# Sparse attention in front of a gated MLP: the probability transposes of 28 jobs on VectorE instead of TensorE, with the scores laid out for it

## The chip, the cores and the metric

The kernel runs on one core of a Trainium2 chip. The core has TensorE (PE in the profile; PEld is its loading of weights), VectorE (DVE), ScalarE (ACT), GpSimd (POOL) and SyncE (SP), which issues most DMAs. Each engine works through its own queue in order. The metric is the device time of one execution in microseconds; the kernel before takes 769.71 us (median of three runs, 769.57 to 770.93).

## The reference

Block-sparse attention over 4 batches, 8 heads, 768 positions and a head dimension of 64, in blocks of 32 positions (24 blocks). Its output feeds an MLP with 512 inputs, 2048 hidden values and a gate `h * relu6(h + 3) / 6`.

```python
scores = scale * np.matmul(q, k.transpose(0, 1, 3, 2))
mask = np.abs(blk_i - blk_j) <= window                     # window = 1 block
mask = mask | (blk_i == 0) | (blk_j == 0) | (blk_i == n_blocks - 1) | (blk_j == n_blocks - 1)
...                                                        # and 3 sampled blocks for each query block
scores = np.where(mask, scores, -1000000000.0)
attn = np.exp(scores - np.max(scores, axis=-1, keepdims=True))
attn = attn / (np.sum(attn, axis=-1, keepdims=True) + 1e-09)
attn_out = np.matmul(attn, v)
...
h = x @ w_in
out = (h * np.clip(h + 3.0, 0.0, 6.0) / 6.0) @ w_out
```

An inner query block sees at most eight key blocks (its neighbours and itself, the first and the last, three sampled). The first and the last query block see all 24.

## The kernel before

**Units of work.** `GROUPS` holds 24 groups: two halves of the batch times 12 pairs of query blocks. Eleven groups of each half are inner pairs; each gives a `Cache` (its eight key and value blocks, loaded into one of two buffers `KP`, `VP`) and two `Job`s, one for each batch of the half: 44 jobs, 22 caches. The remaining group of each half holds the first and the last block and gives four `Dense` jobs. A job makes 64 rows of the MLP's input; eight jobs (four groups) fill 512 tokens, a unit of the MLP. Each unit has 16 `Step`s, one per 128 hidden values, 96 steps in all.

**A job before** (lines 452 to 534). A job has two query blocks `x`, four pairs of heads `t` and the two heads `y` of a pair.

- `s` (462): scores. For each `x`, `t`, `y` one fp32 matmul puts 32 queries times 256 keys (eight key blocks, called slots) into PSUM bank `ps[y]`, at partitions `32t` and columns `256x`: 16 matmuls. In the trace each fp32 matmul is two instructions, `bank<-kp,q`, 64 rows by 32 columns of the array and 256 columns wide.
- `mx` (472): the row maximum, one VectorE reduction for each `y`.
- `e` (479): the exponential on ScalarE, four of them, with the maximum as its bias. It reads slot after slot and writes the columns in the order key within block, slot (`c k s`), so that the transposed tile mixes four slots in one group of 128.
- `t` (486): four 128x128 transposes on TensorE into another PSUM bank (`bank<-ident,p`), for each `y`.
- `ca` or `cv` (491, 495): ScalarE or VectorE copies that to SBUF (`pT`).
- `av` (499): probabilities times values, 16 matmuls for each `y` (`small<-vp,pT`, two instructions each, 128 rows by 32 columns, 65 wide: 64 values and a column of ones that gives the sum).
- `dn`, `ml`, `x` (511 to 523): the reciprocal of the sum, the product, and a VectorE transpose of 32x32 blocks. `xh`, `xl` split the result into a high and a low part for the MLP.

The values of a cache are stored to match: row `4k + s` of `VP` holds key `k` of slot `s` (`values`, 388, `slot % 4::4`).

**A step** (658 to 709). `wh`, `wl` split 128 rows of each weight into a rounded part and the rest (ScalarE, then GpSimd or VectorE). `h` makes the hidden values in two halves of six 128x512 matmuls (`hid`), `ga` (ScalarE), `gb` (VectorE), `gh` (ScalarE) and `gl` (GpSimd) the gate and its split, `o` twelve 128x512 matmuls into the four output banks `OUT`. `hid` has one bank.

**PSUM** has two banks `bank`, one `hid`, one `small` and four `OUT`. The jobs of the first four groups (`early`) also use the `OUT` banks. Scores and transposes of later jobs share the two banks.

**The order** is written out in `SCORE`, a list of phrases such as `j32 s; j33 s; j32 mx_0`: a work, and the operations to issue for it. Every instruction is kept in that order on its engine (`Ordered`, 308; all instructions are recorded there, so the profile shows L316 for nearly all of them). The weights come as 64-bit numbers and are converted by `Weight` (`w` phrases) during the first unit.

Of the kernel before, what the change touches and what calls it, by code (L numbers as in the profile page):

```python
# [10 lines left out]
F32 = mybir.dt.float32  # L11
# [6 lines left out]
P = 128  # L18
# [16 lines left out]
EARLY = 4  # L35
WBUFS = (3, 2)
# [8 lines left out]
    k0 samp_1; q1 load_0; k0 table_1; c0 kg_0; q0 load_1; c1 vw_01; c0 kw_11 vg_0; w1 load_1; c0 kr_111 kr_001; c1  # L45
    kw_11 vw_00 kf_0; c0 vw_01 kw_00; c1 kc_1; k0 index; w0 load_0; c1 kr_000; w1 size; q0 qs_0; c1 kr_010; c0 vw_02
    vw_00; k0 ident_0; c0 vr_01; j1 s; j0 s; j1 mx_0; c0 vr_00; j1 mx_1; c2 kc_0; j0 mx_0; w0 size; j0 mx_1; j1 e_00;
    c1 vr_00; w0 bits_0; j0 e_00 e_01; j1 e_01; j0 e_10; c1 vw_02; j0 e_11; q1 qs_0; w2 load_0; c2 kr_010; j2 s; j0
    t_0 t_1; c2 kr_000; j0 cv_0 ca_1; j1 t_0; j0 av_0; j1 e_10 cv_0 e_11; j0 av_1; j2 mx_0; c2 kw_01; j3 s; j0 dn; j2
    e_00; j0 ml; j2 e_01 mx_1; j1 t_1; c3 kw_01; j3 mx_0; j2 t_0; c1 vg_0; w0 bits_1; q2 load_0; j1 av_0; j2 ca_0; c1  # L50
    vr_01; j3 mx_1; j2 e_10; j1 cv_1; j3 e_00; j2 e_11; w1 bits_0; j1 av_1; j3 e_01; w1 bits_1; w2 size; j2 t_1; c2
    vw_00; w0 bits_2; c3 kr_010; j2 ca_1; j1 dn; j0 x; j3 e_10; j1 ml; w1 bits_2; j1 x; q3 load_0; c2 vw_02; q2 qs_0;
    w4 load_0; m0 wh_0; j4 s; c2 vr_01; j3 e_11; m0 wl_00; j1 xh; m0 wh_1; j2 av_0; j1 xl_1; c2 vw_01; j0 xh; j5 s; c3
    kc_1; c2 vr_00; w2 bits_0; j3 t_0; j5 mx_0; c3 kr_000; j3 t_1; j0 xl_1; j5 e_00; j2 av_1; j4 mx_0 e_00; j2 dn; q3
    qs_0; j2 ml; q4 load_0; j3 ca_0 cv_1; j4 e_01; j3 av_0; w2 bits_1; w4 size; j3 av_1; j2 x; j5 e_01; m0 wl_11; j4
    t_0; c3 vw_00; j4 mx_1; c4 kw_01; j4 ca_0; w3 load_0; j3 dn; j4 e_10; c3 vr_01; w2 bits_2; j4 e_11; j3 ml; j4 t_1;
    j5 mx_1; j4 av_0; c3 vw_01; j4 cv_1; j5 t_0; c3 vw_02; j3 x; c3 vr_00; j6 s; j5 e_10; j2 xh; j5 e_11; j2 xl_0; j5
    ca_0; j4 av_1; c4 kw_00; j6 mx_0; c4 kr_000; j5 t_1; w4 bits_0; j6 e_00; j4 dn; j6 e_01; j7 s; j5 cv_1; j3 xh; w3
    size; j6 mx_1 t_0; c4 kr_010; j4 ml; j6 e_10; j3 xl_1; j5 av_0; j6 ca_0; j7 mx_0; j6 e_11; j5 av_1; w3 bits_0; j7
    e_00; w3 bits_1; j7 e_01; w6 load_0; j7 t_0; w3 bits_2; j6 t_1; j5 dn; j7 mx_1; j4 x; j7 e_10; w4 bits_1; j6 ca_1;  # L60
    q4 qs_0; j5 ml; w4 bits_2; j6 av_0; j7 ca_0; j6 av_1; j5 x; j7 e_11; w5 load_0; j4 xh; j7 t_1; c5 kw_00; j6 dn; j5
    xh; j4 xl_0; c4 vw_01; j6 ml; j7 ca_1; j8 s; w7 load_0; j5 xl_0; j6 x; m1 wh_0; c4 vw_02 vw_00; j7 av_0; j6 xh; m1
    wl_00; j8 mx_0; c4 vr_00; m2 wh_0; j7 av_1; j8 e_00; j7 dn; j8 e_01; j7 ml; j8 t_0; c4 vr_01; j7 x; j6 xl_1; j7
    xh; w6 size; j7 xl_1; j8 mx_1; m0 h_0; w5 size; j8 e_10; w5 bits_0; j8 e_11; w6 bits_0; m0 h_1; m1 wh_1; j8 cv_0;
    m1 wl_11; j8 t_1; m0 ga; w6 bits_1; j8 ca_1; w6 bits_2; j9 s; m0 gb; w9 load_0; q5 load_0; w5 bits_1; m0 gh; m1
    h_0; c5 kw_01; w5 bits_2; w7 size; m0 gl; j9 mx_0; w8 load_0; m1 h_1; c5 kr_000; m2 wl_01; j9 e_00 e_01; w7
    bits_0; m0 o_0; m1 ga; j8 av_0; m1 gb; w9 size; j8 av_1; c5 kr_010; j9 mx_1; m3 wh_0; j9 t_0; m2 h_0; w7 bits_1;
    m3 wl_00; j9 e_10 e_11; w7 bits_2; m1 gh; m0 o_1; m1 gl; m2 h_1; w9 bits_0; w10 load_0; c5 vw_00 vw_01; m0 o_2; j8
    dn; m2 ga; w9 bits_1; m0 o_3; w8 size; w9 bits_2; j9 t_1 ca_0; m1 o_0; j8 ml; w11 load_0; q5 qs_0; j9 cv_1; c5
    vr_01; m1 o_1; w8 bits_0; j10 s; m2 gb; c6 kw_00; m2 gh; j9 av_0; c5 vw_02; j10 mx_0; m2 wh_1; j9 av_1; m2 gl; c5  # L70
    vr_00; j10 mx_1; m1 o_2; w10 size; w8 bits_1; j10 e_00; m1 o_3; j10 e_01; m2 wl_11; j10 e_10; m3 h_0; j10 e_11; w8
    bits_2; w10 bits_0; m4 wh_0; w12 load_0; m3 h_1; j8 x; w11 size; w10 bits_1; j10 t_0; m4 wl_01; m3 ga; m2 o_0; w10
    bits_2; j10 t_1; j9 dn; w14 load_0; m2 o_1; w11 bits_0; j10 ca_1; m3 gb; m2 o_2; j8 xh; j10 ca_0; w11 bits_1; m4
    h_0; m5 wh_0; j9 ml; w11 bits_2; m3 wh_1; j11 s; m3 gh; w13 load_0; c6 kr_010; m3 gl; j10 av_0; j11 mx_0; j10
# [219 lines left out]
def fused_kernel(ctx: ExitStack, tc, qT, kG, vG, vP, kD, vD, sampled, w_in, w_out, table, ident_d, out):  # L294
# [488 lines left out]
```

## Time and profile before

| | |
|---|---|
| median of three runs | 769.71 us |
| the profiled execution | 768.11 us, its span 766.3 us |
| PE / PEld / DVE / ACT / POOL busy | 724.3 / 558.4 / 341.7 / 426.4 / 360.7 us |
| mean granted TensorE clock | 0.994 |
| moved by DMA | 102.52 MB, mean 134 GB/s |
| first `hid` matmul starts at | 70.04 us |
| last matmul ends at | 761.3 us |

The profile gives the busy time of each engine, the span in 40 equal slices (each digit a busy share in tenths), the chain of work that ended last, and groups of instructions: line, engine, operation, what it writes and reads, shapes, count, busy time and the mean duration in ns, then the idle time before them and what ended it. Matmuls overlap, so their durations are longer than their spacing: what one costs is read from the start of one to the start of the next. A timeline row holds start, length, engine, operation and count of instructions merged into one row.

### The profile page before, as it was taken

To read this page: it belongs to the slowest core of one execution; us is meant where nothing else is said; L and a number is where in the kernel's file an instruction comes from. 1 tells how busy PE (TensorE), PEld (TensorE's weight loads), DVE (VectorE), ACT (ScalarE), POOL (GpSimd) and SP (SyncE) were. 2 spreads that over 40 slices of the span, in tenths; PEclk is the share of its full clock that TensorE was granted. 3 is DMA by queue.
4 is the path that set the end of the run, shared out by engine and by line. 5 is a ranking of instruction groups with operands and counts; after the bars stand their busy time and mean duration, and the time that the engine had idled before them with its cause. 6 is when DMAs were issued, how large, how long until landed. Compare 5 with 4: busy or idle time off the path is not lost.

```text
span 766.3 us, 18861 instructions
## 1 busy us (share of the span) xinstructions
PE 724.3 (95%) x7616; PEld 558.4 (73%) x7616; DVE 341.7 (45%) x698; ACT 426.4 (56%) x790; POOL 360.7 (47%) x291
## 2 busy tenths in 40 slices
PE   1577999999999999999999999999999999999997
PEld 0344777777777777777778777777777777888885
DVE  2567989895443434542323334436642133221112
ACT  1567678766565445645656554455654645544441
POOL 0011324355446434455664663442546564676663
PEclk9989999999999999999999999999999999999999
DMA  8688878776361553223451144533442600010001
GB/s 281 199 274 253 284 232 246 239 249 198 122 197 62 169 176 124 64 74 115 153 161 58 35 138 129 179 131 106 133 142 86 207 20 2 1 56 1 0 1 55
DMA packets 57866, 102.52 MB, mean 134 GB/s; under 512 B 7859, under 2 KB 36148, under 8 KB 57780
## 3 DMA queue, kind: packets, MB, share of 16 engines
q1 hardware_dynamic: 56512, 99.62, 41.3%
q10 hardware_dynamic: 1268, 1.71, 0.6%
q8 instruction: 60, 0.98, 0.5%
q14 instruction: 26, 0.21, 0.1%
HBM read 95.00 MB, written 6.29 MB: 132 GB/s over the span
## 4 chain that ended last, share of the span: by engine, by line
PE 89%; SPq 4%; DMA 2%; DVE 2%; ACT 1%; issue 1%; ACTq 0%; POOL 0%; POOLq 0%; DVEq 0%
PE hid L316 35%; PE out L316 34%; PE bank L316 12%; PE small L316 8%; SPq L316 3%; DMA stage<-w_out 1%; ACT p L316 1%; SPq L370 1%; DVE m L316 0%; DMA stage<-w_in 0%; DMA kp<-kG 0%; ACT g L316 0%; DMA vp<-vG 0%; DMA out_dram<-stage 0%; DVE w_in L316 0%
## 5 line engine op out<-in xcount | busy, mean ns | idle before, releaser
L316 PE MATMUL hid<-x,whi 128*128 128x512 f32 x768 | 242.9, 397 | 0.3 <-ACT x L316 0.2
L316 POOL TENSOR_TENSOR glo<-g,ghi 128x512 fp32r<-128x512 f32 x96 | 126.5, 1318 | 181.8 <-ACT ghi L316 163.6
L316 DVE SCALAR_TENSOR_TENSOR g<-g,hid 128x512 f32<-128x512 f32 x96 | 65.8, 686 | 229.8 <-ACT g L316 229.8
L316 PEld LDWEIGHTS hid<-x,whi 128*128 128x128 f32 x768 | 140.6, 188 | 34.6 <-issue 3.2
L316 POOL TENSOR_TENSOR wlo<-w_out,whi 128x512 fp32r<-128x512 f32 x87 | 113.7, 1308 | 98.0 <-ACT whi L316 78.3
L316 PE MATMUL out<-whi,ghi 128*128 128x512 f32 x384 | 159.7, 416 | 0.0
L316 ACT ACTIVATE p<-bank,m 128x256 f32<-128x256 f32 (+1 forms) x192 | 120.8, 691 | 65.1 <-DVE m L316 64.5
L316 POOL TENSOR_TENSOR wlo<-w_in,whi 128x512 fp32r<-128x512 f32 x87 | 113.4, 1308 | 84.3 <-ACT whi L316 79.7
L316 PE MATMUL out<-whi,glo 128*128 128x512 f32 x384 | 150.5, 392 | 0.2 <-POOL glo L316 0.2
L316 PE MATMUL hid<-x,wlo 128*128 128x512 f32 x384 | 150.2, 391 | 0.0
L316 PE MATMUL out<-wlo,ghi 128*128 128x512 f32 x384 | 150.0, 391 | 0.0
L316 ACT ACTIVATE g<-hid,half_b 128x512 f32<-128x512 f32 x96 | 66.1, 688 | 122.8 <-PE hid L316 93.1
L316 DVE TENSOR_REDUCE m<-bank 128x2 f32<-128x512 f32 (+1 forms) x112 | 70.3, 645 | 61.0 <-PE bank L316 60.9
L316 PEld LDWEIGHTS out<-whi,ghi 128*128 128x128 f32 x384 | 72.1, 188 | 22.9 <-issue 9.5
L316 PEld LDWEIGHTS out<-whi,glo 128*128 128x128 f32 x384 | 72.1, 188 | 16.5 <-POOL glo L316 0.6
L316 PEld LDWEIGHTS hid<-x,wlo 128*128 128x128 f32 x384 | 72.1, 188 | 15.8
L316 PEld LDWEIGHTS out<-wlo,ghi 128*128 128x128 f32 x384 | 72.4, 189 | 11.6
L316 ACT CAST whi<-w_out 128x512 fp32r<-128x512 f32 x96 | 60.0, 625 | 32.5 <-PE out L316 29.2
L316 ACT CAST ghi<-g 128x512 fp32r<-128x512 f32 x96 | 60.0, 625 | 31.9 <-DVE g L316 17.2
L316 ACT CAST whi<-w_in 128x512 fp32r<-128x512 f32 x96 | 59.6, 624 | 12.9 <-PE hid L316 8.3
L316 PE MATMUL bank<-ident,p 128*128 128x128 f32 x384 | 58.2, 274 | 2.0 <-ACT p L316 1.7
L316 PEld LDWEIGHTS small<-vp,pT 128*32 128x32 f32 x2816 | 42.6, 110 | 22.9 <-issue 15.3
(59 smaller groups left out, 607.4 us busy)
## 6 DMA issues: line engine op xcount, KB each, us to landing
vp<-vG SPq DMA_DIRECT2D x176, 130.0 KB, 3.4
kp<-kG SPq DMA_DIRECT2D x129, 128.0 KB, 2.8
kp<-kG SPq DMA_DIRECT2D x42, 256.0 KB, 3.6
stage<-w_in SPq DMA_DIRECT2D x16, 512.0 KB, 3.9
stage<-w_out SPq DMA_DIRECT2D x15, 512.0 KB, 4.3
vp<-vP SPq DMA_DIRECT2D x26, 260.0 KB, 3.9
stage<-vD SPq DMA_DIRECT2D x16, 390.0 KB, 4.0
out_dram<-stage SPq DMA_DIRECT2D x24, 256.0 KB, 2.9
```

The lines of the kernel that those rows point to most:

```text
L316: return lambda *a, **k: tc.keep_in_program_order(op(*a, **k))
L370: loads, values = nc.values_load_multi_w_load_instructions(row, engines=[engines[q]], min_val=0, max_val=NB - 1, skip_runtime_bounds_check ...
```

## The change

For jobs 16 to 43 (`n >= TURNED`, 16) the layout of the scores is another. The four slots of a half `c` no longer lie side by side in a row, but on the four groups of 32 partitions: `spread` puts the scores of slots `r` and `r + 4` (`r` from 0 to 3) at partitions `32r` and columns `64(4x + t)`, 32 keys of each slot in their order. A matmul is then 64 columns wide and there are 64 for each job. VectorE's transpose works on blocks of 32x32, so that one instruction for each `y` (`tr`) turns 128x512 probabilities into the layout that `av` needs. The transposes on TensorE, their PSUM bank and the copies `ca`, `cv` are gone for these jobs. The row maximum now spans four groups of partitions: `ms` reduces each group with one operand, `mc` brings the four together with seven small minima (of negated maxima) and spreads the result, `sb` adds it on VectorE from PSUM to SBUF, and `ex` is an exponential in place, without bias, one for each `y`.

The values of their caches (8 to 21) lie in slot order: row `32s + k`. A block pair that was one DMA (`vw_1`, `vg`) is two there.

Jobs 0 to 15 keep the transposes on TensorE. Their score matmuls write the permuted order `c k s` into PSUM (a stride of four elements) and the exponential reads and writes contiguous columns.

`SCORE` is written anew throughout, from its first phrase on. The counts of other operations change little: 11 and 12 of the 96 splits of `w_in` and `w_out` are on VectorE instead of 9 and 9, and three query scalings are on GpSimd instead of one.

```diff
+TURNED = 16
...
         def values(self, slot, step=4):
+            if self.turned:
+                return self.v[slot % 4 * BLK:slot % 4 * BLK + BLK, slot // 4]
             return self.v[slot % 4::step, slot // 4]
+
+        def pair(self, q, slot, pair):
+            if self.turned:
+                for i in range(2):
+                    queues[q].dma_start(out=self.values(slot + 2 * i), in_=self.vP[pair, i::2, :2 * VR])
+            else:
+                queues[q].dma_start(out=self.values(slot, 2), in_=self.vP[pair, :, :2 * VR])
...
         def s(self):
+            if self.turned:
+                self.spread()
+                return
...
-                        pe.matmul(self.ps[y][32 * t:32 * t + 32, 256 * x:256 * x + 256], lhsT=self.group.q[half, t, at:at + 32],
-                                  rhs=self.k[half, 4 * x:4 * x + 8, self.b, BLK * t:BLK * t + BLK], start=True, stop=True)
+                        keys = self.k[half, 4 * x:4 * x + 8, self.b, BLK * t:BLK * t + BLK]
+                        to = self.ps[y][32 * t:32 * t + 32, 256 * x:256 * x + 256]
+                        pe.matmul(to.rearrange("p (c k s) -> p c s k", c=2, s=4), lhsT=self.group.q[half, t, at:at + 32],
+                                  rhs=keys.rearrange("p (c s) k -> p c s k", c=2), start=True, stop=True)
...
-            act.activation(out=self.pr[y][:, half].rearrange("p (c k s) -> p c s k", c=2, s=4),
-                           in_=self.ps[y][:, half].rearrange("p (c s k) -> p c s k", c=2, s=4), func=AF.Exp, bias=self.m[:, 2 * y + x:2 * y + x + 1], scale=1.0)
+            act.activation(out=self.pr[y][:, half], in_=self.ps[y][:, half], func=AF.Exp, bias=self.m[:, 2 * y + x:2 * y + x + 1], scale=1.0)
...
+        def spread(self):
+            self.ps = [bank() for y in range(2)]
+            for x in range(2):
+                at = 64 * self.b + 32 * x
+                for t in range(4):
+                    to = 64 * (4 * x + t)
+                    for r in range(4):
+                        for y in range(2):
+                            half = slice(64 * y, 64 * y + 64)
+                            keys = self.k[half, 4 * x + r:4 * x + r + 5:4, self.b, BLK * t:BLK * t + BLK]
+                            pe.matmul(self.ps[y][32 * r:32 * r + 32, to:to + 64], lhsT=self.group.q[half, t, at:at + 32], rhs=keys,
+                                      start=True, stop=True)
+
+        def ms(self, y):
+            if y == 0:
+                self.m = sb.tile([P, 4, 16], F32, name="mt", bufs=1)
+                self.pr, self.prT = {}, {}
+            dve.tensor_reduce(out=self.m[:, 0, 8 * y:8 * y + 8], in_=self.ps[y].rearrange("p (u n) -> p u n", n=64),
+                              axis=AX.X, op=ALU.max, negate=True)
+
+        def mc(self):
+
+            def least(out, in_):
+                dve.tensor_reduce(out=out, in_=in_, axis=AX.X, op=ALU.min)
+
+            for r in range(1, 4):
+                least(self.m[:32, r], self.m[32 * r:32 * r + 32, 0].rearrange("p (u o) -> p u o", o=1))
+            self.least = sb.tile([P, 16], F32, name="least", bufs=1)
+            least(self.least[:32], self.m[:32].rearrange("p r u -> p u r"))
+            for r in range(1, 4):
+                least(self.least[32 * r:32 * r + 32], self.least[:32].rearrange("p (u o) -> p u o", o=1))
+
+        def sb(self, y):
+            self.pr[y] = sb.tile([P, 512], F32, name="p", bufs=3)
+            m = self.least[:, 8 * y:8 * y + 8].rearrange("p (u o) -> p u o", o=1).to_broadcast([P, 8, 64])
+            dve.tensor_tensor(out=self.pr[y].rearrange("p (u n) -> p u n", n=64), in0=self.ps[y].rearrange("p (u n) -> p u n", n=64),
+                              in1=m, op=ALU.add)
+
+        def ex(self, y):
+            act.activation(out=self.pr[y], in_=self.pr[y], func=AF.Exp)
+
+        def tr(self, y):
+            self.prT[y] = sb.tile([P, 512], F32, name="pT", bufs=3)
+            dve.transpose(out=self.prT[y], in_=self.pr[y])
...
         def av(self, y):
...
-                        pe.matmul(self.us[32 * t:32 * t + 32, at:at + VW], lhsT=self.prT[y][:, (2 * x + c) * P + 32 * t:][:, :32],
+                        col = BLK * (8 * x + 2 * t + c) if self.turned else BLK * (8 * x + 4 * c + t)
+                        pe.matmul(self.us[32 * t:32 * t + 32, at:at + VW], lhsT=self.prT[y][:, col:col + BLK],
```

A stretch of the new `SCORE`, with jobs 40 and 41 in their new form:

```
j40 s; m70 wh_0; m67 o_0; m69 wl_00; j40 ms_0; c21 kw_00; c20 vw_02; m67 o_1; m68 gb; c20 vr_01; m70 wl_00; m67 o_2;
...
j40 ms_1; m68 gl; j38 ml; m69 h_1; j40 mc; m67 o_3; j40 sb_0; m72 wh_0; m69 ga; m68 o_0; j36 xl_1; j40 sb_1;
...
j40 ex_0; m70 gh; m71 h_1; j40 tr_0; m70 gl; j38 x; j41 sb_0; m69 o_0; j41 sb_1; m70 wl_10; m71 ga; m69 o_1; j40 ex_1;
```

More of the change, by code (lines that the diff above doesn't have):

```diff
@@ L50 @@
[L50 to L74, printed above, removed]
@@ new lines @@
+    dn; w3 size; j2 xl_1; j6 mx_0; j5 e_11; c3 vw_02; w3 bits_0; m0 wh_1; j7 s; c3 vr_01; j3 ml; j6 e_00; m0 wl_10; j3
+    x; j6 e_01; j5 cv_0; j4 av_0; c4 kw_01; j6 mx_1; q4 load_0; j4 av_1; w3 bits_1; c4 kw_00; j6 e_10 t_0; c4 kr_000;
+    j6 e_11; j4 dn ml; j6 t_1 ca_0; j4 x; j7 mx_0; j6 ca_1; j7 mx_1; j5 t_1; c4 kr_010; j5 av_0; j7 e_00 e_01; j5
+    cv_1; j4 xh; j7 e_10; w3 bits_2; j4 xl_0; j5 av_1; j3 xh; w6 load_0; j7 t_0 e_11; c5 kw_01; j5 dn; j3 xl_1; q4
+    qs_0; j7 t_1; j5 ml; w4 bits_1; j6 av_0 av_1; j5 x; j7 ca_0 ca_1; j6 dn ml; m1 wh_1; j6 x; j7 av_0; m0 wh_0; w4
@@ new lines @@
+    bits_2; m1 wl_10; j7 av_1; j5 xh; w5 load_0; j7 dn; j8 s; m2 wh_0; j7 ml; c4 vw_01; j6 xh; j5 xl_1; c4 vw_00; j6
+    xl_0; j8 mx_0; w7 load_0; c4 vr_00; m0 wl_00; j7 x; j8 e_00 mx_1 e_01; j7 xh; j8 t_0 e_10; j7 xl_1; w6 size; m0
+    h_0; j8 e_11; w6 bits_0; w5 size; w6 bits_1; j8 t_1 ca_0; m0 h_1; w6 bits_2; j8 ca_1; w5 bits_0; w8 load_0; w5
+    bits_1; c5 kr_000; j9 s; m0 ga gb; j9 mx_0; m1 h_0; m0 gh; q5 load_0; w5 bits_2; j9 e_00; m0 gl; c4 vr_01; w7
+    size; m1 h_1; w7 bits_0; c4 vw_02; j9 mx_1; w8 size; m0 o_0; w9 load_0; w7 bits_1; c5 kw_00; j9 e_01; m0 o_1; c5
@@ new lines @@
+    e_00; j10 x; w14 size; m5 h_1; j11 mx_1; m6 wl_00; j11 e_01; w13 bits_1; j11 e_10; m3 o_2; m5 ga; m3 o_3; j11
+    e_11; w13 bits_2; j11 t_0; w14 bits_0; w17 load_0; j11 t_1 ca_0; m5 gb; q7 load_0; m4 o_0; c6 vw_00; w14 bits_1;
+    m5 gh; m6 h_0; w14 bits_2; w15 size; m5 gl wh_1; w15 bits_0; w16 load_0; m4 o_1; c6 vr_01; j11 ca_1; m4 o_2; m7
+    wh_0; w15 bits_1; j12 s; w15 bits_2; c6 vr_00; w17 size; m6 h_1; m7 wl_01; j12 mx_0; w18 load_0; w17 bits_0; j11
+    av_0; c6 vw_01; j12 e_00; m5 wl_11; m6 ga; j11 av_1; m4 o_3; w17 bits_1; j12 e_01 mx_1 t_0; m5 o_0; m6 gb; j12
@@ new lines @@
+    e_10 e_11; m5 o_1; w17 bits_2; w16 size; m7 h_0; j11 dn; w19 load_0; m6 wh_1; w16 bits_0; j11 ml; m6 gh; w16
+    bits_1; j12 t_1; m6 gl; m5 o_2; j12 cv_0 ca_1; m7 h_1; q7 qs_0; w16 bits_2; w18 size; m6 wl_11; j13 s; j9 xh; w20
+    load_0; j10 xh; c7 kw_01; w18 bits_0; m8 wh_0; j12 av_0; c7 kr_010; w18 bits_1; m7 ga; m8 wl_00; j12 av_1; j13
+    mx_0; m5 o_3; w19 size; m7 gb; m6 o_0; j9 xl_1; m7 gh; c7 kr_000; w19 bits_0; m8 h_0; m7 wh_1; w18 bits_2; m7 gl;
+    j13 e_00 mx_1; m9 wh_0; m8 h_1; w19 bits_1; m7 wl_10; w21 load_0; j12 dn; m6 o_1; w19 bits_2; m8 ga; m6 o_2; m9
@@ new lines @@
+    wl_00; j13 e_01; m8 gb; w20 size; m6 o_3; w22 load_0; c7 kw_00; j11 x; m7 o_0; m8 gh; c7 vr_01; j10 xl_1; w20
+    bits_0; j13 e_10 t_0; m8 gl; j12 ml; m7 o_1; m8 wh_1; w20 bits_1; j13 e_11; m7 o_2; j13 ca_0; m9 h_0; m8 wl_11;
+    w21 size bits_0; j13 t_1; w20 bits_2; m9 h_1; w21 bits_1; m10 wh_0; w23 load_0; w21 bits_2; w22 size; m7 o_3; m9
+    ga; m10 wl_01; w24 load_0; m8 o_0; j13 ca_1; w22 bits_0; m8 o_1; w22 bits_1; m9 wh_1; m8 o_2; w22 bits_2; j14 s;
+    m9 wl_11; m11 wh_0; w25 load_0; c7 vw_01; m9 gb; w23 size; m11 wl_00; j13 av_0; c7 vw_02; j14 mx_0; j13 av_1; m8
@@ new lines @@
+    o_3; w23 bits_0; j14 e_00; w23 bits_1; m9 gh; m10 h_0; w23 bits_2; w24 size; m9 gl; j14 mx_1 e_01; w26 load_0; m10
+    h_1 wh_1; q8 load_0; j12 x; c7 vw_00; w24 bits_0; j14 e_10; c7 vr_00; w24 bits_1; w25 size; m9 o_0; w24 bits_2;
+    m10 ga; j14 t_0; m9 o_1; w27 load_0; m10 gb; c8 vw_00; m9 o_2; j13 dn; m10 gh; w25 bits_0; m11 h_0; j12 xh; j14
+    cv_0; m10 gl; j14 e_11; j13 ml; w26 size; m10 wl_11; m9 o_3; q8 qs_0; w25 bits_1; m11 h_1 wh_1; w26 bits_0; w25
+    bits_2; j14 t_1; m11 ga; m10 o_0; w26 bits_1; w28 load_0; m12 wh_0; w26 bits_2; m10 o_1; j14 ca_1; m12 wl_00; m11
@@ new lines @@
+    gb; j14 av_0; w30 load_0; j11 xh; j14 av_1; m13 wh_0; j15 s; w27 size; m13 wl_01; m11 gh; m10 o_2; j11 xl_1; c9
+    kw_01; j14 dn; m11 gl; j15 mx_0; c8 kr_010; m12 h_0; j15 mx_1 e_00; w28 size; w27 bits_0; m12 h_1; m11 wl_11; j15
+    e_01 e_10; c8 kw_00; w28 bits_0; j15 t_0; w28 bits_1; c8 kw_01; m10 o_3; c8 kr_000; j15 ca_0; w27 bits_1; m11 o_0;
+    w30 size; w27 bits_2; m11 o_1; j15 e_11; w30 bits_0; m12 ga; w30 bits_1; m11 o_2; c8 vw_02; m12 wh_1 gb; j15 t_1;
+    w31 load_0; m11 o_3; c8 vw_01; w28 bits_2; m12 gh; m13 h_0; w30 bits_2; m14 wh_0; m12 gl; c8 vr_01; j13 x; m12
@@ new lines @@
+    wl_11; j13 xh; m13 h_1; m15 wh_0; m13 wh_1; j14 ml; m12 o_0; j12 xl_1; j15 ca_1; m14 wl_01; j15 av_0; m13 ga; j14
+    x; j15 av_1; m13 gb; j16 s; c9 vw_02; m15 wl_01; m13 gh; w29 load_0; m14 h_0; c9 kr_010; j13 xl_1; m13 gl; j16
+    ms_0 ms_1; m14 h_1; j15 dn; m13 wl_10; j16 mc; c8 vg_0; m12 o_1; m14 ga; c8 vr_00; m12 o_2; m16 wh_0; m14 gb; m12
+    o_3; m16 wl_00; j16 sb_0; m15 h_0; m14 gh; q9 load_0; j15 ml; j16 sb_1; w31 size; m14 gl; j15 x; m15 h_1; c9
+    vr_01; w29 size; j16 ex_0; w29 bits_0; w31 bits_0; j14 xh; j17 s; c9 kr_000; w29 bits_1; m15 ga; j14 xl_0; w31
@@ L396, in vw @@
             if i == 1:
-                queues[q].dma_start(out=self.values(4, 2), in_=self.vP[self.g, :, :2 * VR])
+                self.pair(q, 4, self.g)
             else:
@@ L406, in vg @@
         def vg(self, q):
-            queues[q].dma_start(out=self.values(5, 2), in_=self.vP[11, :, :2 * VR])
+            self.pair(q, 5, 11)
         def copy(self, engine, out, in_):
```

394 lines of the change are left out of this document (189 added, 205 removed).

## The prediction

> **What bounds the kernel now.** I read the page first (busy shares, slices, the chain), then the windows, the PE waits, and the PE timeline around single jobs.
>
> ```profile
> PE 724.3 (95%) x7616; PEld 558.4 (73%) x7616; DVE 341.7 (45%) x698; ACT 426.4 (56%) x790; POOL 360.7 (47%) x291
> PE   1577999999999999999999999999999999999997
> PEclk9989999999999999999999999999999999999999
> PE 89%; SPq 4%; DMA 2%; DVE 2%; ACT 1%; issue 1%; ACTq 0%; POOL 0%; POOLq 0%; DVEq 0%
> ```
>
> TensorE is busy from the fourth slice to the end at a full granted clock, and the chain that ended last runs through PE for 89% of the span. The windows (columns: stretch, length, busy time of PE, PEld, DVE, ACT, POOL, clock, DMA share, GB/s) place the exception:
>
> ```profile
> 0.00:70.00 70.00, 34.60 (x868) 22.09 (x868) 35.34 (x86) 37.10 (x70) 4.99 (x10) 0.95 0.79 250
> 70.00:150.00 80.00, 79.58 (x911) 60.89 (x912) 71.03 (x125) 59.55 (x108) 26.24 (x19) 1.00 0.79 252
> 150.00:590.00 440.00, 439.24 (x4668) 337.24 (x4667) 195.44 (x413) 248.32 (x469) 224.88 (x180) 1.00 0.42 130
> ```
>
> In the first 70 us nothing is full except the loads, at 250 GB/s; after that PE misses 0.4 us of 80 and 0.8 us of 440. The PE waits from 70 us on say the same:
>
> ```profile
> PE bank L316 <- ACT p L316: 0.6, 2, 0.5
> PE bank L316 <- ACT pT L316: 0.3, 1, 0.3
> ```
>
> So behind 70 us a microsecond that PE no longer has to work is a microsecond off the time, as long as the others keep up. All 28 changed jobs (16 to 43) lie there. The price of each piece is what it adds between two full-size matmuls (128x512), which follow each other at 2.72 / 12 = 0.227 us:
>
> ```profile
> 702.35 2.72 PE hid L316 x12
> ```
>
> **Transposes taken off PE.** A transpose piece (`t`, four 128x128) between full-size matmuls:
>
> ```profile
> 654.18 0.39 PE L316 MATMUL out<-whi,glo 128*128 128x512 f32 x1
> 654.41 0.60 PE L316 MATMUL bank<-ident,p 128*128 128x128 f32 x4
> 654.77 0.47 PE L316 MATMUL out<-whi,ghi 128*128 128x512 f32 x1
> 655.08 0.39 PE L316 MATMUL out<-wlo,ghi 128*128 128x512 f32 x1
> ```
>
> From 654.18 to 655.08 are 0.90 us, of which two full-size matmuls account for 0.45; the piece costs 0.447 us (0.36 of its own, the rest in the slower start of the next matmul). 28 jobs x 2 pieces x 0.447 = 25.0 us, all on the path. **-25.0 us**, the largest term.
>
> **Four times as many score matmuls, a quarter as long.** This is the disputed term. A job's scores go from 16 matmuls of 256 columns (32 rows in the trace, each fp32 matmul being two) to 64 of 64 columns (128 rows). The array is divided the same way, 64 rows by 32 columns, eight tiles. The nearest rows are the scores and values of one job, and a narrow matmul of the dense jobs:
>
> ```profile
> 630.29 0.39 PE L316 MATMUL hid<-x,wlo 128*128 128x512 f32 x1
> 630.61 1.11 PE L316 MATMUL small<-vp,pT 128*32 128x65 f32 x64
> 631.65 1.09 PE L316 MATMUL bank<-kp,q 64*32 64x256 f32 x32
> 632.68 0.50 PE L316 MATMUL out<-whi,ghi 128*128 128x512 f32 x1
> 633.01 0.39 PE L316 MATMUL out<-wlo,ghi 128*128 128x512 f32 x1
> 468.89 0.64 PE L316 MATMUL small<-ident,xq 128*32 128x64 f32 x16
> 469.46 0.88 PE L316 MATMUL bank<-stage,q 64*64 64x384 f32 x8
> ```
>
> From start to start: scores, 32 in 1.03 us, 32.2 ns each, 256 columns over eight tiles, which is 1.01 ns per column of one tile. Values, 64 in 1.04 us, 16.25 ns each, 65 columns over four tiles: 1.00 ns. The narrow one, 16 in 0.57 us, 35.6 ns each, 64 columns over the two column groups that the code writes: 1.11 ns. Three shapes obey one rule, time = columns / tiles x 1.0 to 1.1 ns; doubling the tiles at the same width halved the spacing (35.6 to 16.25), so no per-instruction limit shows down to 16 ns. By that rule a new score matmul takes 64 / 8 x 1.0 = 8.0 ns and a job 128 x 8.0 = 1.02 us, against 1.03 now; at 1.11 it is 1.14. The other end is that 16.25 ns, the closest spacing the trace has, is a floor: 128 x 16.25 = 2.08 us, +1.05 per job, +29.4 in all. I take the rule, since three rows lie on it and none shows a floor, nearer its lower end: +0.05 x 28 = **+1.4 us**; ends 0 and +29.4.
>
> The page TensorEngine Tiling (Array Packing) of the Trainium skill, section Instruction Overhead, speaks against this edit: each matmul has about 60 cycles of overhead, so a tiling factor should not be taken from a dimension that is already small. With the 2.4 GHz that the skill's page Trainium Kernel Development and Optimization gives for TensorE (NeuronCore Architecture), an estimate from both is 25 ns a matmul, 3.2 us a job, +61 us in all. Read as a floor for each instruction, the trace disagrees already (16.25 ns); read as a floor for each tile, 64 columns just reach it and the edit is free.
>
> **The order on PE.** Entering and leaving a group of small matmuls costs too. Values and scores together: 633.01 - 630.29 - 0.454 = 2.27 us, 0.20 above their 2.07. Values alone:
>
> ```profile
> 661.22 0.40 PE L316 MATMUL out<-whi,glo 128*128 128x512 f32 x1
> 661.55 1.11 PE L316 MATMUL small<-vp,pT 128*32 128x65 f32 x64
> 662.59 0.72 PE L316 MATMUL hid<-x,whi 128*128 128x512 f32 x2
> 663.16 0.40 PE L316 MATMUL hid<-x,wlo 128*128 128x512 f32 x1
> ```
>
> 1.94 - 3 x 0.227 = 1.26 us, again 0.21 above 1.04. In the old list one of the 28 jobs has its scores away from any values; in the new list seven do. 6 x 0.21 = **+1.3 us**.
>
> **Work moved to VectorE.** Durations of the nearest rows:
>
> ```profile
> L316 DVE TENSOR_REDUCE m<-bank 128x2 f32<-128x512 f32 x80 | 53.5, 682 | 27.5 <-PE bank L316 27.4
> L316 DVE SCALAR_TENSOR_TENSOR g<-g,hid 128x512 f32<-128x512 f32 x96 | 65.8, 686 | 229.8 <-ACT g L316 229.8
> L316 DVE STREAM_TRANSPOSE xt<-xq 128x256 f32<-128x256 f32 x44 | 19.1, 434 | 0.7 <-POOL x L316 0.4
> L316 DVE RECIPROCAL rec<-rec 128x4 f32<-128x4 f32 x44 | 7.8, 178 | 1.5
> L316 DVE TENSOR_TENSOR f<-f,m 128x2 f32<-128x2 f32 x16 | 9.0, 564 | 0.6
> L316 DVE COPY pT<-bank 128x512 f32<-128x512 f32 x24 | 16.5, 688 | 24.3 <-PE bank L316 24.2
> L316 DVE TENSOR_SCALAR rec<-small 128x4 f32<-128x4 f32 x44 | 6.7, 153 | 17.8 <-PE small L316 17.8
> L316 DVE TENSOR_TENSOR xq<-small,rec 128x256 f32<-128x256 f32 x44 | 18.4, 419 | 0.7
> L316 DVE TENSOR_TENSOR x<-xt,x 128x256 fp32r<-128x256 f32 x29 | 14.7, 507 | 14.2 <-ACT x L316 14.1
> ```
>
> Per job: the two maxima stay (0.68 each, as many elements read). Added: two adds of the maximum out of PSUM, 2 x 0.69; two transposes 128x512, between 0.68 (what any 512-wide pass takes) and 0.87 (twice the 434 ns), I take 0.75; seven tiny minima in `mc`, 7 x 0.178 = 1.25 from the reciprocal of 4 columns, at the far end 7 x 0.564 = 3.95. Removed: a share of the copies at 0.69. Net about +3.9 us a job, some 105 us over stretches in which VectorE is 44% busy (195 of 440). On average it is hidden; where jobs crowd it may not be. Between the scores of job 32 and the first matmul of step 64, which needs the results of jobs 32 to 35, the new list holds 40.3 us of PE work by the prices above, and 37.5 us of VectorE work, each of its operations taken at the row that fits it (26.5 in the old list, where PE had 44.7). Between the first matmuls of steps 0 and 16 both engines have about 109 us in the new list, and DVE was already busy 71 of 80 us there. So a little is lost: I take **+2 us**, ends 0 and +11 (below, second rival). What queues behind a late `mc` on VectorE is `gb`, and behind it `gh`, `gl` and PE's output matmuls.
>
> **ScalarE.**
>
> ```profile
> L316 ACT ACTIVATE p<-bank,m 128x256 f32<-128x256 f32 x160 | 103.0, 713 | 46.9 <-DVE m L316 46.5 <-DVE rec L316 0.2
> L316 ACT ACTIVATE p<-bank,m 128x384 f32<-128x384 f32 x32 | 17.9, 580 | 18.2 <-DVE m L316 18.0
> L316 ACT COPY pT<-bank 128x512 f32<-128x512 f32 x48 | 28.3, 589 | 11.3 <-PE bank L316 11.2
> ```
>
> A changed job drops four exponentials of 713 ns and its ScalarE copies for two of about 0.69 us, near 2 us less. In jobs 0 to 15 the exponential becomes contiguous: 384 contiguous columns take 580 ns where 256 strided take 713, so about 0.47. Behind 70 us this engine is not late, so: 0. Those jobs' score matmuls now write PSUM at a stride of four elements; no row shows that. It could be free, or as slow as half speed, +1.03 us for each of the 8 jobs behind the first 70 us, +8. I take 0, since the three rows above follow columns and tiles and nothing else; the +8 is kept as a rival.
>
> **The first 70 us.** They are paced by loads at 250 GB/s. Ahead of the first hidden matmul the new list issues one window load and one group of three sampled loads of values fewer:
>
> ```profile
> vp<-vG SPq DMA_DIRECT2D x176, 130.0 KB, 3.4
> ```
>
> 4 x 130 KB = 0.52 MB = 2.1 us, and the exponentials there are shorter. But the whole opening is in a new order, on two queues. **-1.5 us**, ends -6 and +4. The values of changed caches cost one or two more DMA issues each on SP, whose queue has room.
>
> **Sum** against the profiled execution, 768.1 us: -25.0 + 1.4 + 1.3 + 2 - 1.5 = -21.8, so 746.3. That execution lies 1.6 us under the median of 769.7; the forecast for a median is 747.
>
> **The rivals.**
> *VectorE sets the pace where jobs crowd.* If the seven minima cost 0.56 each, as the `f` row has it, each job takes 2.7 us more: in the stretch of four jobs ahead of step 64 that is 37.5 + 5 x 2.7 = 51 against 40.3, 10.7 us of PE idle; jobs 22 to 30 reach 74 + 9 x 2.7 = 98 against 97 of PE, about 1. Total 747 + 10 = 757. For it: the 564 ns. Against: the small operations that end a job take 153 and 178, and its sum is still below PE's everywhere at that price.
> *A floor per matmul* (slower). The mechanism: PE's supply of instructions cannot go closer than the 16.25 ns of the values' matmuls, so a job's scores take 2.08 us. 746.3 + 29.4 - 1.4 = 774, with the median's offset 775. It decides from (21.8 + 1.4) / 28 = 0.83 us more per job, 1.86 us, 14.5 ns a matmul. For it: no row is closer than 16.25. Against: the spacing follows columns and tiles. The page TensorEngine Tiling (Array Packing) of the Trainium skill would, by its 25 ns, give 806; at 16.25 ns seen, I leave that reading 0.02 of this rival's chance.
> *The opening or the strided writes cost.* 747 + 8 = 755.
> *The saving returns as waits*, the rest being ordered to what PE did before: about 769, no change. Against it: the order is new throughout.
>
> **How the numbers follow.** Forecast 0.60, VectorE 0.20, opening or writes 0.07, floor 0.10, no change 0.03. The time is the forecast's. The range 738 to 764 holds the first three: its low end takes the opening's best end and VectorE at 0, its high end the VectorE case with part of another cost; the floor is left out. Differences below 0.2% (1.5 us) are no change for this measurement: faster 0.86, same 0.03, slower 0.11.
>
> **What would show it.** Right: 128 rows `bank<-kp,q` of 64x64 per changed job spanning 1.0 to 1.15 us; 160 transposes 128x128 in place of 384 to bank; PE still without waits behind the first hidden matmul, and busy some 24 us less; DVE near 440 us. Wrong: these rows spanning 2 us; new PE waits on DVE of some microseconds between steps 59 and 64; a first hidden matmul well after 70 us.

## The result and the profile after

The changed kernel takes 776.28 us (median of five, 774.45 to 778.34) against 769.91 us of the kernel before (median of five in the same comparison). The ratio is 1.0078, with a 95% interval of 1.0056 to 1.0101: slower by 0.8%, where 747 us was forecast. The profiled execution took 775.86 us, its span 773.8 us, which is 7.5 us above the span before.

From the page of the kernel after, the busy times, the slices of PE and the chain, and from its third part the queue that brings instructions (packets, MB, share):

```profile
PE 719.5 (93%) x10080; PEld 568.4 (73%) x10080; DVE 427.0 (55%) x991; ACT 366.8 (47%) x697; POOL 355.5 (46%) x287
PE   2777999989999999999998999998999899999997
q8 instruction: 79, 1.29, 0.7%
PE 90%; issue 3%; DMA 2%; DVE 2%; SPq 2%; ACT 0%; POOL 0%; POOLq 0%; DVEq 0%; ACTq 0%
```

and the same queue in the kernel before:

```profile
q8 instruction: 60, 0.98, 0.5%
```

PE is busy 4.8 us less, not 24 us, and its slices are no longer all 9. The chain has 3% of "issue", time in which PE waited for nothing that the profile shows. The instruction queue tells how PE's program arrives: 79 packets for 20160 matmuls and weight loads, 60 for 15232, about 255 for each. So PE's instructions come in blocks of 256, and the change added 19 blocks.

The windows and the PE waits behind 70 us:

```profile
70.00:150.00 80.00, 79.46 (x889) 61.90 (x888) 70.44 (x129) 55.56 (x108) 24.54 (x17) 1.00 0.80 263
150.00:590.00 440.00, 423.97 (x6604) 334.34 (x6603) 257.56 (x637) 205.73 (x392) 216.76 (x174) 1.00 0.45 132
```

```profile
PE bank L316 <- issue: 14.8, 8, 3.2
PE small L316 <- issue: 4.0, 3, 1.4
PE hid L316 <- DVE g L316: 0.5, 1, 0.5
```

In the middle stretch PE now misses 16 us of 440 where it missed 0.8. The waits name neither VectorE nor ScalarE: 18.8 us stand under "issue", in eleven pieces, all inside groups of small matmuls; VectorE has held PE up once, for 0.5 us.

A changed job's scores by themselves, in PE's timeline of the kernel after:

```profile
202.06 0.39 PE L316 MATMUL hid<-x,wlo 128*128 128x512 f32 x1
202.38 1.48 PE L316 MATMUL bank<-kp,q 64*32 64x64 f32 x128
203.80 0.50 PE L316 MATMUL out<-whi,ghi 128*128 128x512 f32 x1
204.14 0.40 PE L316 MATMUL out<-wlo,ghi 128*128 128x512 f32 x1
```

204.14 - 202.06 - 0.454 = 1.62 us, where 1.02 + 0.21 = 1.23 was expected. Two windows of that group (scores alone) show how: the first counts 32 matmuls in 0.25 us, the second the rest.

```profile
202.38:202.63 0.25, 0.25 (x32) 0.25 (x33) 0.00 (x0) 0.00 (x0) 1.00 0.86 328
202.63:203.65 1.02, 1.02 (x125) 1.02 (x103) 0.00 (x0) 0.00 (x0) 1.00 0.14 46
```

(A window counts those that are still under way at its start: the second holds 96 new starts.) The first 32 go at 7.8 ns each, the rate that the prediction's rule gives. The last 96 need about 1 us, 10 ns each. So the array does at first what was forecast; that it stops doing so because a stock of instructions is used up is a guess at this point.

Scores beside values, with one of the waits:

```profile
402.42 0.39 PE L316 MATMUL hid<-x,wlo 128*128 128x512 f32 x1
402.74 1.12 PE L316 MATMUL small<-vp,pT 128*32 128x65 f32 x64
403.79 1.02 PE L316 MATMUL bank<-kp,q 64*32 64x64 f32 x78
407.21 0.73 PE L316 MATMUL bank<-kp,q 64*32 64x64 f32 x50 [2.40 <-issue]
407.87 0.50 PE L316 MATMUL out<-whi,ghi 128*128 128x512 f32 x1
408.20 0.40 PE L316 MATMUL out<-wlo,ghi 128*128 128x512 f32 x1
```

PE stops in the middle of one job's scores, after 78 of 128 matmuls, with every operand there, and goes on 2.4 us later. The whole group takes 5.33 us (408.20 - 402.42 - 0.454).

**Two theories.** *Supply*: PE gets a matmul and its weight load no faster than every 10 ns or so once its stock is used up, and a block of 256 instructions has to be there when the one before is used up. Scores and values of a changed job are 384 instructions, one and a half blocks, in 2.5 us where nothing waits; before they were 192. Where a border falls badly, the next block comes too late. *Hand-offs*: the array is slow with narrow matmuls, or the new work on VectorE and the new order hold PE up, and "issue" is only where the profile puts it.

### The profile page after: what moved, and what is told of

It is laid out like the page before. It is cut to its first block, busy times and chain, and to the rows that moved or that the text cites. A ratio compares the mean times of both kernels' runs of the same rounds, so it can differ in the third digit from the quotient of the medians.

```text
span 773.8 us, 23987 instructions
## 1 busy us (share of the span) xinstructions
PE 719.5 (93%) x10080; PEld 568.4 (73%) x10080; DVE 427.0 (55%) x991; ACT 366.8 (47%) x697; POOL 355.5 (46%) x287
## 4 chain that ended last, share of the span: by engine, by line
PE 90%; issue 3%; DMA 2%; DVE 2%; SPq 2%; ACT 0%; POOL 0%; POOLq 0%; DVEq 0%; ACTq 0%
PE out L316 36%; PE hid L316 35%; PE bank L316 11%; PE small L316 8%; SPq L316 2%; DMA kp<-kG 1%; DVE m L316 1%; DMA ident<-ident 0%; DVE w_in L316 0%; DMA vp<-vG 0%; DMA out_dram<-stage 0%; SPq L370 0%; DVE xq L316 0%; DVE stage L316 0%; DVE w_out L316 0%
## 5 line engine op out<-in xcount | busy, mean ns | idle before, releaser
L316 POOL TENSOR_TENSOR wlo<-w_out,whi 128x512 fp32r<-128x512 f32 x84 | 109.4, 1303 | 157.0 <-ACT whi L316 137.4
L316 PEld LDWEIGHTS hid<-x,whi 128*128 128x128 f32 x768 | 142.3, 189 | 33.8 <-issue 2.4
L316 PE MATMUL out<-whi,ghi 128*128 128x512 f32 x384 | 158.0, 412 | 0.0
L316 POOL TENSOR_TENSOR wlo<-w_in,whi 128x512 fp32r<-128x512 f32 x85 | 110.5, 1306 | 48.8 <-ACT whi L316 40.0
L316 PE MATMUL bank<-kp,q 64*32 64x64 f32 (+1 forms) x3968 | 60.0, 246 | 30.7 <-DMA kp<-kG 15.9
L316 PEld LDWEIGHTS out<-wlo,ghi 128*128 128x128 f32 x384 | 72.7, 189 | 12.8
L316 PEld LDWEIGHTS bank<-kp,q 64*32 64x32 f32 x3968 | 44.6, 106 | 43.8 <-issue 37.7
L316 PEld LDWEIGHTS small<-vp,pT 128*32 128x32 f32 x2816 | 45.2, 114 | 27.8 <-issue 21.3
L316 PE MATMUL small<-vp,pT 128*32 128x65 f32 x2816 | 53.6, 229 | 12.4 <-DVE xq L316 4.2
```

The costliest lines, as they stand in the source:

```text
L316: return lambda *a, **k: tc.keep_in_program_order(op(*a, **k))
```

## Experiments

### Ten bursts of other widths

The kernel after, with this behind its end for ten shapes (columns, tile height and width); nothing reads the results.

```diff
+    def probe(count, cols, height, width):
...
+        for i in range(count):
+            where = i % (P // height * (P // width))
+            row, col = where % (P // height), where // (P // height)
...
+            pe.matmul(to[row][width * col:width * col + width, at:at + cols], lhsT=q[rows, i // 8 % 4, :width],
+                      rhs=flat[rows, at:at + cols], start=True, stop=True)
```

> The kernel after, with ten bursts of 128 matmul rows added behind its end (64 fp32 matmuls each, nothing reads them), a few full-size matmuls ahead of each. Supply theory (TensorE gets a matmul and its weight load no faster than about 10 ns once its queue is used up): over eight tiles 256 columns 32 ns a row, 128 columns 16, 96 columns 12, and 64, 32 and 16 columns all about 10 ns; over four tiles 65 columns 16.3, 32 and 16 columns about 10. Column theory (time is columns by tiles): 64 columns 8 to 10, 32 columns 4 to 5, 16 columns 2 to 3; over four tiles 32 columns 8, 16 columns 4. The time itself is not compared.

PE's timeline of five of the bursts, three over eight tiles and two over four (each burst runs to the start of the row behind it; the rows 128x512 are the full-size matmuls between the bursts):

```profile
824.47 1.59 PE L316 MATMUL bank<-kp,q 64*32 64x64 f32 x128
826.11 10.57 PE L316 MATMUL bank<-kp,ident 128*128 128x512 f32 x24
836.61 1.40 PE L316 MATMUL bank<-kp,q 64*32 64x32 f32 x128
838.05 10.57 PE L316 MATMUL bank<-kp,ident 128*128 128x512 f32 x24
848.55 1.37 PE L316 MATMUL bank<-kp,q 64*32 64x16 f32 x128
849.98 10.57 PE L316 MATMUL bank<-kp,ident 128*128 128x512 f32 x24
...
860.48 2.03 PE L316 MATMUL bank<-kp,q 128*32 128x65 f32 x128
862.44 10.57 PE L316 MATMUL bank<-kp,ident 128*128 128x512 f32 x24
872.94 1.30 PE L316 MATMUL bank<-kp,q 128*32 128x32 f32 x128
874.16 10.57 PE L316 MATMUL bank<-kp,ident 128*128 128x512 f32 x24
```

Over eight tiles, 16, 32 and 64 columns take 1.43, 1.44 and 1.64 us, entry and exit included: 11.2, 11.3 and 12.8 ns each; the wider ones, not shown, 14.7 (96), 17.2 (128) and 30.5 (256). Over four tiles 32 columns take 9.5 ns, 65 take 15.3. A quarter of the columns saves an eighth of the time: there is a floor near 10 ns for a matmul with its weight load, which the column theory (4 to 5 and 2 to 3 ns) does not have. Whether the floor is the delivery of the two instructions or the weight load itself, these bursts cannot tell; that 32 of them ran at 7.8 ns, loads included, speaks for delivery but does not show it.

### The narrow scores alone, in the kernel before

```diff
+            parts = 4 if self.n >= 16 else 1
+            cols = 256 // parts
...
+                for r in range(parts):
+                    slots = slice(4 * x + r * cols // BLK, 4 * x + (r + 1) * cols // BLK)
+                    to = 256 * x + r * cols
...
-                        pe.matmul(self.ps[y][32 * t:32 * t + 32, 256 * x:256 * x + 256], lhsT=self.group.q[half, t, at:at + 32],
+                            pe.matmul(self.ps[y][32 * t:32 * t + 32, to:to + cols], lhsT=self.group.q[half, t, at:at + 32],
```

> The kernel before with one part of the change alone: the scores of jobs 16 to 43 as 64 matmuls of 64 columns, written to the same places as before; transposes, order and VectorE's work stay as they were. Supply theory: +0.39 us for each of 28 jobs (11 us), and waits of 1 to 3 us where scores and values follow each other and a block of 256 instructions runs out, together 10 to 25 us: 785 to 806 us. Rival (the loss comes from VectorE's added work or from the new order): 770 to 773 us.

820.74 us (four runs, 813.32 to 825.51), ratio to the kernel before 1.0655 (1.0615 to 1.0696). One edit, in which VectorE and the order of the work are as before, costs about 50 us, more than supply was thought to. Its PE waits:

```profile
PE small L316 <- issue: 16.1, 10, 2.9
PE bank L316 <- issue: 9.6, 8, 2.1
```

Here nearly all jobs have scores and values side by side, and 26 us of issue come on top of 28 x 0.39 = 11 us. These 37 us are most of the 43 us that the profiled execution spent more than before behind its first hidden matmul. The other 6 us are waits too: read from start to start, the 25 groups of a changed job's scores beside 64 matmuls of values take 97.9 us, where 25 x 2.66 = 66.5 would do without waits (2.66 us is such a group in the kernel after when nothing waits). That is 31.4 us lost, more than the 26 under issue, since a wait is counted only from the modelled end of the matmul before it. The rival is out.

### Scores and values apart

The order on PE of the kernel after is changed where a changed job's scores stand beside a job's values, 21 times, at job 24 for example so (`h_0` and `o_1` are nine full-size matmuls):

```diff
-    j22 av_1; m33 wl_10; j24 s; m31 oc_2; m33 gh; j23 tr_0; m31 od_2; m34 h_0; m33 gl; c12 vw_00; j24 ms_0; c13 kr_010; m31 oc_3; m32 o_1;
+    j22 av_1; m33 wl_10; m34 h_0; m32 o_1; j24 s; m31 oc_2; m33 gh; j23 tr_0; m31 od_2; m33 gl; c12 vw_00; j24 ms_0; c13 kr_010; m31 oc_3;
```

> The kernel after with another order on TensorE alone: where the scores of a changed job and a job's values stood side by side, 9 to 12 full-size matmuls (2 to 2.7 us) now stand between them; every operation is the same. Supply theory: TensorE's waits for issue fall from 19 us to under 4, 21 more entries and exits cost about 0.2 us each: 758 to 764 us, below the kernel before. Rival (the waits are hand-offs of banks and results between VectorE and TensorE, or VectorE's queue): the waits stay, 774 us or more.

780.55 us (six runs, 779.11 to 782.00), 1.0116 (1.0090 to 1.0141). In this order the values products of jobs 17 and 27 come behind a load that replaces some of their values, so those two read other values, and the time is touched by it too (below). Its PE waits:

```profile
PE hid L331 <- DVE g L331: 8.8, 14, 1.4
PE small L331 <- DMA vp<-vP: 4.1, 1, 4.1
PE small L331 <- issue: 1.4, 2, 1.1
PE bank L331 <- issue: 1.1, 2, 0.6
```

Half of the expectation held: the waits for issue fell from 18.8 to 2.5 us. The time did not follow, because the order was paid for elsewhere. Scores that come later keep VectorE waiting in their maxima, and the gates of the MLP, which stand behind them in its queue, come late (8.8 us in 14 waits). The 4.1 us are a fault of this order: job 27's products stop after 8 of 64 matmuls for the load of values that it puts ahead of them. With 21 entries at 0.2 us these pieces are about as much as the 16.3 us of issue that went; the stretch from the first hidden matmul to the end grew by 5.6 us all the same, and about 5 us of that stay open. As a test of the time it decides nothing; as a test of the waits it speaks for supply.

### The same program, moved by half a block, by a whole one, and in the kernel before

Three kernels differ from the kernel after, or the kernel before, by two lines: 32 fp32 matmuls of one column (each is two matmul and two weight load instructions, 128 in all) or 64 (256), ahead of everything, when PE has nothing to do for more than 10 us.

```diff
     nc.gpsimd.memset(half_b, 0.5)
+    for i in range(32):
+        pe.matmul(OUT[3][0:1, 0:1], lhsT=half_b, rhs=half_b, start=True, stop=True)
```

Half a block, in the kernel after:

> The kernel after with 32 matmuls of one column ahead of everything, in time in which TensorE has nothing to do: 128 instructions, half a block of 256, are put ahead of the rest and nothing else changes. Supply theory: the borders of the blocks fall elsewhere, so other groups wait: those at 367, 555, 612 and 631 us, which have no wait now, get waits of 1 to 3 us, several of those that wait now lose theirs, and the time moves by 2 to 15 us either way. Rival (hand-offs between engines): the same groups wait for the same times, and the time stays within 2 us of 776.

767.06 us (ten runs, 764.00 to 773.31), ratio to the kernel before 0.9946 (0.9921 to 0.9971). More work on PE, 9 us less time than the kernel after. The group shown above, in this kernel:

```profile
399.50 0.39 PE L316 MATMUL hid<-x,wlo 128*128 128x512 f32 x1
399.82 1.12 PE L316 MATMUL small<-vp,pT 128*32 128x65 f32 x64
400.87 1.48 PE L316 MATMUL bank<-kp,q 64*32 64x64 f32 x128
402.28 0.50 PE L316 MATMUL out<-whi,ghi 128*128 128x512 f32 x1
402.62 0.39 PE L316 MATMUL out<-wlo,ghi 128*128 128x512 f32 x1
```

and a group that had no wait in the kernel after (at 611.65 there):

```profile
599.05 1.12 PE L316 MATMUL small<-vp,pT 128*32 128x65 f32 x64
600.10 1.14 PE L316 MATMUL bank<-kp,q 64*32 64x64 f32 x93
602.61 0.54 PE L316 MATMUL bank<-kp,q 64*32 64x64 f32 x35 [1.37 <-issue]
```

The first went from 5.33 to 2.66 us, the second gained a wait. So it is nearly throughout: of the ten groups of the kernel after that lost over 1 us each, seven lose nothing here and one 0.3 us (two still wait); five that lost nothing lose 0.9 to 1.8 us. Of the four that were named as new ones only the one at 612 does; the one at 555 loses 0.6 us, the other two 0.3 us and nothing, so the places were not yet known well. The waits for issue sum to 11.1 us instead of 18.8.

A whole block, in the kernel after:

> The kernel after with 64 one-column matmuls (256 instructions, a whole block) ahead. Supply theory: every border falls where it fell in the kernel after, so the same groups wait for the same times (166, 337, 352, 382, 403, 416, 517, 534, 546, 598 us) and the time is that of the kernel after, 774 to 778 us. Rival (extra matmuls help, more of them more): 767 us or less.

777.27 us (four runs, 774.24 to 778.98), 1.0074 (1.0049 to 1.0099): back to the time of the kernel after. All ten groups named wait again, though not for the same times (1.1 to 2.4 us each, where it was 0.9 to 3.2), and no other loses over 0.6 us; 17.1 us of issue. The effect of instructions put ahead repeats with 256.

Half a block, in the kernel before:

> The kernel before with the same 32 one-column matmuls (128 instructions) ahead of everything. Supply theory: no group here uses up a block of 256 instructions in under some 4 us (scores and values together are 192 instructions in 2 us), so the borders of the blocks do not matter: 770 us, within 1.5 us, no waits for issue on TensorE behind 70 us. Rival (the extra matmuls help by themselves, as an early start of the clock or of the opening): faster by several us, as the changed kernel was.

768.41 us (ten runs, 767.75 to 773.14), 0.9980 (0.9966 to 0.9994). PE waits for nothing under issue behind 70 us; the 0.2% is far from the 9 us. The extra matmuls do not help by themselves.

### How often a block comes

The kernel after, with longer bursts behind its end.

```diff
-    for shape in ((64, 256, 64, 32), ...
+    for shape in ((512, 64, 64, 32), (512, 16, P, 32), (64, 64, 64, 32)):
         probe(*shape)
```

> The kernel after with two bursts of 1024 matmul rows behind its end (512 fp32 matmuls; with their weight loads 2048 instructions, eight blocks of 256), 64 columns over eight tiles and 16 columns over four, then one of 128 rows. If the next block is asked for only when a border is crossed and needs some 4 us, each of the later blocks takes about 4 us: 28 to 34 us a burst, with a wait for issue of 2 to 3 us every 128 rows, the same for both widths. If blocks come faster than they are used and the waits had another reason: 10 to 11 us a burst at the floor of 10 ns, without waits. If they come at some rate between, the spacing of the waits gives it.

PE's timeline of the two bursts, 64 columns over eight tiles and 16 over four:

```profile
779.09 2.77 PE L316 MATMUL bank<-kp,q 64*32 64x64 f32 x249
783.81 1.47 PE L316 MATMUL bank<-kp,q 64*32 64x64 f32 x128 [1.94 <-issue]
787.55 2.04 PE L316 MATMUL bank<-kp,q 64*32 64x64 f32 x128 [2.27 <-issue]
791.30 2.04 PE L316 MATMUL bank<-kp,q 64*32 64x64 f32 x128 [1.70 <-issue]
...
826.98 1.91 PE L316 MATMUL bank<-kp,q 128*32 128x16 f32 x128 [2.21 <-issue]
830.72 1.90 PE L316 MATMUL bank<-kp,q 128*32 128x16 f32 x128 [1.84 <-issue]
```

After the first 249 matmuls PE stops and from then on gets exactly 128 matmuls, with their weight loads a block of 256, every 3.74 us, whatever the width. This is the mechanism by itself: about two blocks are on hand, and blocks used up faster than one in 3.74 us leave PE standing. A changed job's scores and values use one and a half in 2.5 us; whether they wait is a matter of where in a block they begin, which is what the moved programs showed.

The traces also hold the start and the length of every packet of the instruction queue, though no view lists them. In the first burst PE goes on at 783.81 us, a packet starts 1.18 us later and lasts 1.25 us, and PE goes on with the next block 1.32 us after its end, at 787.55; the next packet starts 1.17 us behind that. These three pieces make up the 3.74 us: the next block is fetched only once PE has gone on into the one before it. In the kernel after, each of the eleven waits for issue ends 1.3 to 1.6 us after the end of such a packet; for the wait shown above, which ended at 407.21, the packet ran from 404.77 to 405.87. So these waits are for instructions and not for another engine.

### A chosen place, and the five groups that are left

From the places at which groups waited in the kernels with 0 and 128 instructions ahead, 148 were chosen; the second kernel also sets five groups apart.

```diff
+    for i in range(37):
+        pe.matmul(OUT[3][0:1, 0:1], lhsT=half_b, rhs=half_b, start=True, stop=True)
```

> The kernel after with 37 one-column matmuls (148 instructions) ahead. From the places in a block at which groups waited in the two kernels with 0 and 128 instructions ahead (scores and values side by side wait when they begin some 65 to 165 instructions behind a listed border), five such groups should wait here instead of ten and eight, 8 to 10 us in all instead of 19.6 and 11.9: 763 to 766 us. Rival (no rule in the places): anywhere between 767 and 776.

769.60 us (twelve runs, 766.53 to 777.10), 0.9989 (0.9960 to 1.0018). The five groups named are those that wait (0.9 to 2.2 us each); beside them one job's scores alone wait 0.8 us and a full-size matmul 1.0, in all 9.8 us of issue, as expected. The time is not: its opening is slow, the first hidden matmul starts at 73.5 us and not at 70.0 as in the kernel after. From there to the end it takes 692.7 us, against 703.8 of the kernel after and 693.3 with 128 ahead.

> As the kernel with 148 instructions ahead, and for the five groups that should still wait (scores of jobs 18, 21, 32, 34, 41) 9 to 12 full-size matmuls are put between scores and values on TensorE; one gate step goes ahead of job 41's maximum. Supply theory: their waits go, five entries more cost 0.2 us each, VectorE's gates may come late once or twice: 756 to 762 us, the fastest here. Rival (the waits are of the crowded places and come back in another form): no faster than the kernel with 148 alone.

761.43 us (six runs, 761.09 to 769.18), 0.9914 (0.9879 to 0.9948): faster than both kernels. Its waits for issue on PE:

```profile
PE out L332 <- issue: 2.0, 2, 1.9
...
PE bank L332 <- issue: 0.9, 2, 0.5
```

The five waits went; 2.9 us of issue remain, 1.9 of them in one wait of a full-size matmul. From the first hidden matmul to the end it takes 687.2 us, 9.1 less than the kernel before (696.3). That is the sum with few waits: -25.0 for transposes, +11.0 for scores at the floor, +1.3 for groups that stand alone in the kernel after, +1.0 for five more, +2.9 of issue make -8.8. That it closes to 0.3 us is in part luck, since none of its terms is known that well.

## Why the prediction was wrong

**The step that failed** is "Four times as many score matmuls, a quarter as long", where +1.4 us was taken between ends of 0 and +29.4. It cost 30 us or more: 28 x 0.39 = 11.0 us at the floor of 10 ns, and 18.8 us of waits for blocks (some 22 when read from start to start). The rule, columns by tiles, held for the first 32 of the 128 new matmul rows of a group and for no more of them. The error was to let three rows that all lie above 16 ns speak for 8 ns, and to leave out of the sum that PE's program has to be brought in, in blocks, while the edit quadruples its score matmuls; supply stood only in a rival, as a floor for each matmul. Part 3 of the page had the blocks in one line, 60 packets for PE's 15232 instructions. The far end, 16.25 ns as a floor, gave 775 us; that it is close to the measured time is luck: the floor is 10 ns, and the larger part of the loss is a block that is not there yet.

*The rivals.* "A floor per matmul" had the right place and sign and was given 0.10. VectorE's rival did not occur. The 25 ns estimated from the page TensorEngine Tiling (Array Packing) of the Trainium skill are not seen: 10 ns is the measured floor over several tiles. Its advice, not to tile a dimension that is already small, fits the result.

*Transposes*, -25.0 us: their count fell as foreseen, from 384 to 160 in the banks. Their rows before and after:

```profile
L316 PE MATMUL bank<-ident,p 128*128 128x128 f32 x384 | 58.2, 274 | 2.0 <-ACT p L316 1.7
L316 PE MATMUL bank<-ident,p 128*128 128x128 f32 x160 | 24.3, 273 | 1.7 <-ACT p L316 1.7
```

No run takes the transposes away alone, but the price can be read in the trace before: of the 57 pieces of four that stand alone behind the first hidden matmul, 51 take 0.44 to 0.47 us and six take 0.5 to 1.15, so that they were worth some 2 us more than the forecast took.

*Order*, +1.3 us: seven jobs' scores stand alone at 1.62 us, values alone at 1.25, together 2.66 when nothing waits; 0.21 for each as priced.

*VectorE*, +2 us: it was nothing. The durations were close, and no PE wait on it is longer than 0.5 us. Its rows in the kernel after:

```profile
L316 DVE STREAM_TRANSPOSE pT<-p 128x512 f32<-128x512 f32 x56 | 38.7, 697 | 9.0 <-ACT p L316 8.3 <-PE small L316 0.2
L316 DVE TENSOR_REDUCE least<-least 32x16 f32<-32x16 f32 x84 | 13.5, 160 | 1.8
L316 DVE TENSOR_REDUCE mt<-mt 32x16 f32<-32x16 f32 x84 | 13.3, 158 | 1.6
L316 DVE TENSOR_REDUCE least<-mt 32x16 f32<-32x64 f32 x28 | 7.1, 254 | 1.0
```

A transpose takes 0.70 us (0.75 taken), the seven minima 3 x 0.158 + 0.254 + 3 x 0.160 = 1.21 us (1.25 taken).

*ScalarE*, 0: the contiguous exponential takes 474 ns as worked out, and nothing came of it on the path. *Strided score writes*, 0: score matmuls of jobs 0 to 15 cost the same beside values behind 70 us, 2.27 us.

*The opening*, -1.5 us: 0. The first hidden matmul starts at 70.0 us in both kernels, half a megabyte less or not; in the kernels made from this one it lies between 68.2 and 73.5 us, for reasons not followed up.

Together -25.0 + 11.0 + 18.8 + 1.3 = +6.1, against +7.5 us of span. The waits are counted from the modelled end of a matmul, which takes some 0.3 us off each of eleven, and the slower transposes work the other way; both together leave about +8.

## What to carry to other kernels

Count instructions as well as columns: where small matmuls are cut up further, ask how many instructions they put into a few microseconds; here TensorE got 256 in 3.74 us, and the packets of the instruction queue count the blocks. A price that lies below every row of the trace is an extrapolation, and its range should reach to the nearest row. When PE stops inside a group with "issue" as the reason, putting half a block of idle instructions ahead of the program is a cheap test, and a whole block its control: if other groups stop with the half and the old ones with the whole, it is the supply.

## What the runs showed of the hardware

PE's program comes in blocks of 256 instructions (79 packets, 20160 instructions). A group of 384 in 2.5 us can leave it without instructions for 0.3 to 3.2 us (the eleven waits of the kernel after); one of 192 in 2 us never did in the kernel before. The page Runtime: NRT & Kernel Launch of the Trainium skill, section Instruction fetch mechanics, has the blocks, and that crossing one is mostly hidden: the trace agrees on the size, and shows 18.8 us that are not hidden. In a long run of small matmuls a block comes every 3.74 us: its packet starts 1.1 to 1.2 us after PE went on into the block before, lasts 1.0 to 1.3 us, and PE goes on 1.2 to 1.5 us after its end.

A matmul with its weight load goes no faster than about 10 ns in a burst over several tiles, however few its columns (9.4 to 11.3 ns at 16 and 32), and took 7.8 ns for the first 32 of a group in the kernel after. What sets these 10 ns is open.

Two programs that differ by 32 idle matmuls differ by 9 us in 770. The place of a program in its instruction blocks is part of its time, and a verdict of under 2% on a kernel of this kind holds for that place only.
